# Attention scores in a tuned attention and two-FFN kernel: 64 row by 32 column matmuls in four corners of the array

## The chip, the cores and the metric

The kernel runs on one core of a Trainium2 chip. The core has a matrix engine (TensorE, PE in the profile, with its weight loads as PEld), three engines for elementwise work (VectorE or DVE, ScalarE or ACT, GpSimd or POOL), and SyncE (SP), which here only issues the transfers between main memory (HBM) and on-chip memory (SBUF). Matmuls write to PSUM, which holds 8 banks of 128 partitions by 512 float32 values. The metric is the device time of one execution in microseconds (us).

## The reference

The attention is in chunks of 32 queries. Each chunk sees 8 memory slots, 16 positions to the left, its own 32 and 8 to the right, 64 keys in all. Two feed-forward layers follow, on 3072 tokens of width 512.

```python
for c in range(S // 32):
    k_full = concatenate([mem_k, k[c_start - 16 : c_end + 8]])      # 64 keys, cut at the ends
    scores = scale * q_c @ k_full.T                                 # 32 x 64 per head and chunk
    a = exp(scores - max(scores)); a = a / (sum(a) + 1e-9)
    out_c = a @ v_full
x = attn_out.reshape(3072, 512)
x = relu(x @ moe_w_in) ** 2 @ moe_w_out                             # 512 -> 2048 -> 512
x = silu(x @ w_gate) * (x @ w_val) @ w_out                          # 512 -> 1536 -> 512
```

There are 4 batches, 8 heads, 768 positions and a head width of 64. The inputs are float32.

## The kernel before

The attention is cut into 24 units. A unit is 128 positions of one batch (4 chunks) with all 8 heads, so 32 pairs of a head and a chunk. The host lays out queries, keys (already windowed to 64 per chunk) and values as one block of 128 partitions by 1024 values (512 KB) for each unit. The query block holds two heads on its partitions, 64 rows each, and the columns of a pair of heads are laid out as a block diagonal: 32 columns that are zero in the lower 64 rows and 32 columns that are zero in the upper 64. One matmul of 128 rows by 64 columns thus gives the scores of two heads of a chunk at once, because the zeros keep the two heads apart.

A unit goes through these steps, each a method of `Unit`:

- `__init__` issues the transfers of `q`, `k`, `v` on SP (L525).
- `scores` (L529, matmul in L544) is 16 float32 matmuls into one PSUM bank. Even ones write the partitions 0 to 63, odd ones 64 to 127, so the stationary operands alternate between two column halves of the array.
- `weigh` is the softmax: maximum (L573), subtraction (L578) and sum (L589) on VectorE, the exponential on ACT (L585), the scaling (L603) on POOL or VectorE.
- `turn_pe` (L644, for the first 8 units) or `turn` (L622) transposes the weights into a block-diagonal buffer.
- `mixing` (L673) is the weighted sum, 16 float32 matmuls of the same tile shape as those of the scores.
- `leave` splits the result into a high and a low float32r part (L467, L474) for the first layer.

From the tenth unit on, the weighted sum of one unit and the scores of the next are one planned step: `scores(after)` calls that unit's `mixing()` first. The first layer (L852) and the output of the first layer (L879) are full-size matmuls (128 by 128, 512 moving columns, 12 for each block). The units are spread among them up to about 410 us. After that the second layers (L1108, L1245) follow, without attention.

The order of the work on each engine is not written out by hand. `Plan.run` simulates the engines with costs that are given with every step (`{"PE": 1.16}` for scores alone, `{"PE": 2.2}` with a weighted sum) and with a cost `move` for the bytes of a transfer, and sets the instructions in the order in which this simulation starts them. So a changed `move` can change the order on every engine. Transfers stand in one queue on SP; each waits for the eighth before it.

Of the kernel before, what the change touches and what calls it, by code (L numbers as in the profile page):

```python
# [17 lines left out]
P = 128  # L18
B, H, S, D = 4, 8, 768, 64
CH, LEFT, RIGHT, NMEM = 32, 16, 8, 8  # L20
WIN = NMEM + LEFT + CH + RIGHT
UPB = S // P
NU = B * UPB
# [293 lines left out]
def rate(nbytes):  # L317
    return nbytes / 370e3
# [3 lines left out]
def tile_chunked_attention_two_ffn(ctx: ExitStack, tc, qd, kd, vd, w1, w2, wo2, out):  # L322
# [63 lines left out]
    def at(b):  # L386
        name, n = home(b)
        if name in ("RP", "W1"):
            return wide[name, n]
        if name == "R" and n >= sizes["R"]:  # L390
            n -= sizes["R"]
            if n < 2 * sizes["RP"]:
                return wide["RP", n // 2][:, 1024 * (n % 2) : 1024 * (n % 2) + 1024]
            n -= 2 * sizes["RP"]
            return homes["X"][n // 4][:, 1024 * (n % 4) : 1024 * (n % 4) + 1024]
        return homes[name][n]
# [121 lines left out]
    class Unit:  # L518
        def __init__(self, u, pool, start):
            self.u, self.start = u, start  # L520
            self.q, self.k, self.v = (pl.buf(pool, n) for n in "qkv")
            srcs = [(self.q, qd), (self.k, kd), (self.v, vd)]
            for b, src in srcs:
                pl.op(
                    {"SP": 0.4}, lambda b=b, src=src: nc.sync.dma_start(out=at(b), in_=src[u]),  # L525
                    (), (b,), move=rate(524288),
                )

        def scores(self, after=None):  # L529
            u, sc = self.u, pl.buf("PS", "sc")  # L530
            self.sc = sc
            mixing, reads, writes = after.mixing() if after else (None, (), ())

            def run():
                if mixing:
                    mixing()
                q = at(self.q).rearrange("p (s m c q) -> p s m c q", s=2, m=2, c=4)
                k = at(self.k).rearrange("p (s m c k) -> p s m c k", s=2, m=2, c=4)
                o = at(sc).rearrange("p (s f m k) -> p s f m k", s=2, f=2, m=2)
                for p in range(4):  # L540
                    s, m = p // 2, p % 2
                    for ci in range(4):
                        f, par = ci // 2, ci % 2
                        nc.tensor.matmul(  # L544
                            o[64 * par : 64 * par + 64, s, f, m, :], q[:, s, m, ci, :],
                            k[:, s, m, ci, :], start=True, stop=True,
                        )

            pl.op(
                {"PE": 2.2 if after else 1.16}, run, (self.q, self.k, *reads), (sc, *writes), tail=0.2  # L550
            )

            def edge(r, f, a, b):
                o = at(sc).rearrange("p (s f m k) -> p s f m k", s=2, f=2, m=2)
                nc.vector.memset(o[r : r + 64, :, f, :, a:b], NEG)

            if u % UPB == 0:
                pl.op({"DVE": 0.11}, lambda: edge(0, 0, NMEM, NMEM + LEFT), (), (sc,))
            if u % UPB == UPB - 1:
                pl.op({"DVE": 0.11}, lambda: edge(64, 1, WIN - RIGHT, WIN), (), (sc,))  # L560
# [910 lines left out]
def _layout(q, k, v, mem_k, mem_v, moe_w_in, moe_w_out, moe2_w_gate, moe2_w_val, moe2_w_out):  # L1471

    f = np.float32
    nch = S // CH

    def windows(a, mem):
        pad = np.zeros((B, H, LEFT + S + RIGHT, D), f)
        pad[:, :, LEFT : LEFT + S] = a
        w = np.empty((B, H, nch, WIN, D), f)
        for c in range(nch):  # L1480
            w[:, :, c, :NMEM] = mem
            w[:, :, c, NMEM:] = pad[:, :, c * CH : c * CH + WIN - NMEM]
        return w

    kw, vw = windows(k, mem_k), windows(v, mem_v)

    q8 = q.reshape(B, 2, 2, 2, UPB, 4, CH, D)
    qz = np.zeros((B, UPB, 2, D, 2, 2, 4, 2, CH), f)
    for hh in range(2):
        qz[:, :, hh, :, :, :, :, hh, :] = q8[:, :, :, hh].transpose(0, 3, 6, 1, 2, 4, 5)  # L1490
    k8 = kw.reshape(B, 2, 2, 2, UPB, 4, WIN, D)
    kk = k8.transpose(0, 4, 3, 7, 1, 2, 5, 6)
    v8 = vw.reshape(B, 2, 2, 2, UPB, 4, WIN, D)
    vv = v8.transpose(0, 4, 2, 6, 3, 1, 5, 7)

    def cols(w, nf):
        return w.reshape(KC, P, nf, P).transpose(2, 1, 0, 3).reshape(nf, P, KC * P)

    w1 = np.concatenate([cols(moe_w_in, NF1), moe_w_out.reshape(NF1, P, DM)], axis=2)
    w2 = np.stack([cols(moe2_w_gate, NF2), cols(moe2_w_val, NF2)], axis=1)  # L1500

    wo2 = moe2_w_out.reshape(NF2 // 2, 2, P, 2, DM // 2).transpose(0, 3, 2, 1, 4)
    return {
        "q": qz.reshape(NU, P, 1024),
        "k": kk.reshape(NU, P, 1024),
        "v": vv.reshape(NU, P, 1024),
        "w1": w1.view(np.int64),
        "w2": w2.view(np.int64),
        "wo2": np.ascontiguousarray(wo2).reshape(NF2 // 2, 2, P, DM).view(np.int64),
    }  # L1510
# [19 lines left out]
```

## Time and profile before

| | us |
|---|---|
| median of 3 runs | 1105.41 |
| lowest, highest | 1105.08, 1106.93 |
| the profiled execution's own time | 1106.09 |
| span of its trace | 1104.3 |
| PE busy | 1082.3 (98%) |
| VectorE busy | 860.0 (78%) |
| ACT busy | 594.1 (54%) |
| HBM read, written | 227.02 MB, 81.26 MB |

The span is the time from the first to the last instruction of the program on the core; the execution's own time has some 1.8 us around it. A busy share is an average over the span. Matmuls are pipelined, so the duration of a single one in the trace is longer than the time by which it delays the next, and what a block of them costs is read from start to start.

### The profile page before, as it was taken

What the parts mean: (1) busy time and instruction counts of PE and PEld (TensorE: products, weight loads), DVE (VectorE), ACT (ScalarE), POOL (GpSimd) and SP (SyncE); (2) the same over time, 40 slices, a digit from 0 to 9 for tenths busy, and PEclk for the clock granted to TensorE, in tenths of its full rate; (3) what the DMA queues carried; (4) which work ended last, traced back from release to release, by engine and by line L of the source; (5) the groups of instructions that cost most, each with busy time, mean ns of one, the idle gap of its engine ahead of it and who ended that gap; (6) DMA issues with size and microseconds to landing.
All of it is one profiled execution on the core that took longest, in us unless ns stands there. A gap on an engine that the chain in (4) does not pass through costs nothing.

```text
span 1104.3 us, 17051 instructions
## 1 busy us (share of the span) xinstructions
PE 1082.3 (98%) x6044; PEld 892.0 (81%) x6044; DVE 860.0 (78%) x1540; ACT 594.1 (54%) x1010; POOL 126.5 (11%) x106
## 2 busy tenths in 40 slices
PE   5899999999999999999999999999999999999998
PEld 4778888888888888888888888888888887888886
DVE  6999878878879999778997667998769854534981
ACT  4888554554556566556654344564566633333650
POOL 2113101112011222001300000102310000000000
PEclk9899999999999999999999999999999999999999
DMA  9953487888889889999868999996998578655552
GB/s 362 409 222 113 134 278 242 296 294 300 306 277 344 288 285 342 393 344 348 290 225 266 404 406 395 328 357 224 358 335 298 161 241 307 213 195 172 190 169 99
DMA packets 133669, 309.42 MB, mean 280 GB/s; under 512 B 13136, under 2 KB 50000, under 8 KB 133584
## 3 DMA queue, kind: packets, MB, share of 16 engines
q1 hardware_dynamic: 133584, 308.33, 78.9%
q8 instruction: 48, 0.79, 0.3%
q14 instruction: 37, 0.30, 0.1%
HBM read 227.02 MB, written 81.26 MB: 279 GB/s over the span
## 4 chain that ended last, share of the span: by engine, by line
PE 95%; DMA 2%; ACT 1%; DVE 1%; issue 0%; SPq 0%; ACTq 0%
PE ps L1108 37%; PE ps L1245 22%; PE ps L852 16%; PE ps L879 15%; PE ps L673 2%; PE ps L544 2%; DMA rp0float<-in_w 1%; DMA s<-in_q 1%; ACT f L765 0%; SPq L525 0%; DVE u L486 0%; PE ps L644 0%; ACT f L772 0%; DVE f L486 0%; DVE rp3float32r L815 0%
## 5 line engine op out<-in xcount | busy, mean ns | idle before, releaser
L495 ACT ACTIVATE t<-ps 128x512 f32<-128x512 f32 x170 | 100.9, 596 | 218.4 <-PE ps L852 102.3
L486 DVE TENSOR_TENSOR t<-t,ps 128x512 f32<-128x512 f32 x72 | 49.1, 686 | 42.0 <-PE ps L1108 38.1
L622 DVE STREAM_TRANSPOSE a<-t 32x128 f32<-32x128 f32 x256 | 77.4, 303 | 4.3
L495 ACT ACTIVATE t<-t 128x512 f32<-128x512 f32 x72 | 45.3, 632 | 57.8 <-DVE t L486 57.4
L486 DVE TENSOR_TENSOR u<-u,u 128x512 f32<-128x512 f32 x70 | 48.2, 711 | 0.1
L474 POOL TENSOR_TENSOR r<-t,r 128x512 fp32r<-128x512 f32 x21 | 29.8, 1420 | 147.8 <-ACT r L467 107.8
L467 ACT ACTIVATE f<-f 128x512 fp32r<-128x512 f32 (+1 forms) x60 | 32.4, 546 | 15.3 <-DVE f L486 10.2
L474 DVE TENSOR_TENSOR f<-f,f 128x512 fp32r<-128x512 f32 (+1 forms) x52 | 32.7, 631 | 9.6 <-ACT f L467 9.2
L474 DVE TENSOR_TENSOR r<-t,r 128x512 fp32r<-128x512 f32 x32 | 22.1, 689 | 22.6 <-ACT r L467 22.5
L486 DVE TENSOR_TENSOR u<-ps,t 128x512 f32<-128x512 f32 x26 | 17.9, 689 | 26.5 <-PE ps L1108 24.9
L495 ACT ACTIVATE u<-ps 128x512 f32<-128x512 f32 x45 | 26.7, 595 | 20.6 <-PE ps L1108 20.3
L866 ACT ACTIVATE t<-t 128x512 f32<-128x512 f32 x56 | 35.3, 630 | 1.3
L467 ACT ACTIVATE r<-t 128x512 fp32r<-128x512 f32 x53 | 33.3, 629 | 1.5 <-DVE t L869 0.2
L486 DVE TENSOR_TENSOR u<-ps,u 128x512 f32<-128x512 f32 x34 | 23.4, 689 | 9.4 <-PE ps L1108 8.8
L585 ACT ACTIVATE t<-t 128x512 f32<-128x512 f32 x24 | 15.1, 630 | 22.3 <-DVE t L578 22.3
L673 PEld LDWEIGHTS ps<-a,a 128*64 128x64 f32 x640 | 20.3, 138 | 6.7 <-issue 4.9
L673 PE MATMUL ps<-a,a 128*64 128x64 f32 x640 | 23.0, 225 | 0.0
L544 PE MATMUL ps<-a,a 128*64 128x64 f32 x640 | 22.3, 223 | 0.0
L802 DVE CUSTOM_DVE_ANT_0 f<-f,f 128x2048 uint16<-128x2048 uint16 (+1 forms) x17 | 22.0, 1294 | 0.3
L544 PEld LDWEIGHTS ps<-a,a 128*64 128x64 f32 x640 | 20.4, 138 | 1.8 <-issue 1.4
L474 POOL TENSOR_TENSOR rp9float32r<-u,rp9float32r 128x512 fp32r<-128x512 f32 x2 | 5.9, 2972 | 127.2 <-ACT rp9float32r L467 115.9
L467 ACT ACTIVATE x<-u 128x512 fp32r<-128x512 f32 x26 | 16.3, 626 | 7.6 <-PE ps L1245 4.2
(836 smaller groups left out, 3096.9 us busy)
## 6 DMA issues: line engine op xcount, KB each, us to landing
tma<-f SPq DMA_DIRECT2D x31, 512.0 KB, 5.8
f<-in_w SPq DMA_DIRECT2D x21, 512.0 KB, 5.5
a<-in_q SPq DMA_DIRECT2D x20, 512.0 KB, 5.6
a<-in_k SPq DMA_DIRECT2D x20, 512.0 KB, 6.7
a<-in_v SPq DMA_DIRECT2D x20, 512.0 KB, 4.3
rp0float32r<-tma SPq DMA_DIRECT2D x14, 512.0 KB, 6.2
rp3float32r<-tma SPq DMA_DIRECT2D x12, 512.0 KB, 5.9
rp2float32r<-tma SPq DMA_DIRECT2D x11, 512.0 KB, 6.6
```

What stands on the lines that cost most here:

```text
L467: lambda: nc.scalar.activation(out=dst(HI), in_=src(), func=AF.Copy),
L474: eng.tensor_tensor(out=dst(LO), in0=src(), in1=dst(HI).bitcast(F32), op=ALU.subtract)
L486: eng.tensor_tensor(out=out[1](), in0=x[1](), in1=y[1](), op=op)
L495: nc.scalar.activation(out=out[1](), in_=x[1](), func=func)
L544: nc.tensor.matmul(o[64 * par : 64 * par + 64, s, f, m, :], q[:, s, m, ci, :], k[:, s, m, ci, :], start=True, stop=True,)
L622: nc.vector.transpose(out=o[g : g + 32, hh, :, :, m, :].rearrange("k s (f c) q -> k s f c q", c=2)[:, :, :, par, :], in_=a[r : r + 32, :, ...
L673: nc.tensor.matmul(o[64 * hh : 64 * hh + 64, 2 * s : 2 * s + 2, CH * ci : CH * ci + CH], a[:, hh, s, ci, :], b[:, hh, s, ci].rearrange("p ...
L852: nc.tensor.matmul(at(hp), w1of("in", i, a)[:, k * P : k * P + P], x[:, b, k, :], start=(n == 0), stop=(n == len(terms) - 1),)
L866: nc.scalar.activation(out=at(h), in_=at(h), func=AF.Square)
L879: nc.tensor.matmul(at(accs[m]), w1of("out", i, a)[:, m * P : m * P + P], at(h2)[:, 512 * b : 512 * b + 512], start=(i == 0 and n == 0), st ...
L1108: nc.tensor.matmul(at(bank), at(w[slot])[:, o : o + P], at(r[i, n])[:, 512 * b : 512 * b + 512], start=(first and n == 0 and m == 0), stop ...
L1245: nc.tensor.matmul(at(bank[i][n]), at(w[i][g // 2])[:, o : o + P], at(r)[:, 512 * b : 512 * b + 512], start=(first and m == 0), stop=(g == ...
```

## The change

The query block loses its zeros. It is now 128 partitions by 512 values (256 KB): the 64 rows of one head on the upper partitions, those of the other below, 32 columns for each chunk. The 16 score matmuls become 32, one for each head and chunk, with 64 rows and 32 columns. `tile_position=(r, g)` places each in one of four pieces of the array: rows 0 or 64, columns 0, 32, 64 or 96, so that the four that follow each other lie at (0, 0), (64, 32), (0, 64) and (64, 96). The scores land where they landed before. The planner's cost for the bytes of a query block is halved; its costs for the score step are as before.

```diff
             for b, src in srcs:
                 pl.op(
-                    {"SP": 0.4}, lambda b=b, src=src: nc.sync.dma_start(out=at(b), in_=src[u]),
-                    (), (b,), move=rate(524288),
+                    {"SP": 0.4}, lambda b=b, src=src: nc.sync.dma_start(out=at(b)[:, : src.shape[-1]], in_=src[u]),
+                    (), (b,), move=rate(262144 if src is qd else 524288),
                 )
...
-                q = at(self.q).rearrange("p (s m c q) -> p s m c q", s=2, m=2, c=4)
+                q = at(self.q)[:, :512].rearrange("p (s m c q) -> p s m c q", s=2, m=2, c=4)
                 k = at(self.k).rearrange("p (s m c k) -> p s m c k", s=2, m=2, c=4)
                 o = at(sc).rearrange("p (s f m k) -> p s f m k", s=2, f=2, m=2)
-                for p in range(4):
-                    s, m = p // 2, p % 2
-                    for ci in range(4):
-                        f, par = ci // 2, ci % 2
-                        nc.tensor.matmul(
-                            o[64 * par : 64 * par + 64, s, f, m, :], q[:, s, m, ci, :],
-                            k[:, s, m, ci, :], start=True, stop=True,
-                        )
+                for n in range(32):
+                    (s, m), f, par, hh = divmod(n // 8, 2), n // 4 % 2, n // 2 % 2, n % 2
+                    r, g = 64 * hh, 64 * par + 32 * hh
+                    nc.tensor.matmul(
+                        o[g : g + 32, s, f, m, :], q[r : r + 64, s, m, 2 * f + par, :],
+                        k[r : r + 64, s, m, 2 * f + par, :], start=True, stop=True,
+                        tile_position=(r, g),
+                    )
...
-    qz = np.zeros((B, UPB, 2, D, 2, 2, 4, 2, CH), f)
-    for hh in range(2):
-        qz[:, :, hh, :, :, :, :, hh, :] = q8[:, :, :, hh].transpose(0, 3, 6, 1, 2, 4, 5)
+    qq = q8.transpose(0, 4, 3, 7, 1, 2, 5, 6)
...
-        "q": qz.reshape(NU, P, 1024),
+        "q": qq.reshape(NU, P, 512),
```

The order on PE moves with it. This is its head before the change, from behind the third score block on. A row is a line of the kernel, the operation, output from inputs, the size of the output, and how often; L544 (L543 in the changed kernel) are the scores, L644 transposes, L673 weighted sums, L852 the first layer, `s` and `a` the tiles of queries, keys and values.

```order
L644 MATMUL ps_91<-ident,t_77 128x128 x4
L544 MATMUL ps_92<-s_193,s_192 64x64 x16
L673 MATMUL ps_93<-a_67,s_194 64x2x32 x16
L644 MATMUL ps_94<-ident,t_78 128x128 x4
L673 MATMUL ps_95<-a_68,s_195 64x2x32 x16
L644 MATMUL ps_88<-ident,t_79 128x128 x4
L644 MATMUL ps_89<-ident,t_80 128x128 x4
L673 MATMUL ps_90<-a_67,s_196 64x2x32 x16
L673 MATMUL ps_91<-a_68,s_197 64x2x32 x16
L852 MATMUL ps_92<-xx,rp9float32r 128x512 x12
L852 MATMUL ps_94<-xx,rp9float32r 128x512 x12
L544 MATMUL ps_93<-a_70,a_69 64x64 x16
```

And this is the same place on PE now, from the third score block down to the first full-size block.

```order
L543 MATMUL ps_90<-s_191,s_190 32x64 x32
L543 MATMUL ps_91<-s_193,s_192 32x64 x32
L644 MATMUL ps_92<-ident,t_77 128x128 x4
L644 MATMUL ps_93<-ident,t_78 128x128 x4
L673 MATMUL ps_94<-a_67,s_194 64x2x32 x16
L673 MATMUL ps_95<-a_68,s_195 64x2x32 x16
L644 MATMUL ps_88<-ident,t_79 128x128 x4
L644 MATMUL ps_89<-ident,t_80 128x128 x4
L673 MATMUL ps_90<-a_67,s_196 64x2x32 x16
L673 MATMUL ps_91<-a_68,s_197 64x2x32 x16
L543 MATMUL ps_92<-a_70,a_69 32x64 x32
L852 MATMUL ps_93<-xx,rp9float32r 128x512 x12
```

The fourth score block has moved ahead of the first transpose, and the fifth, which stood behind two blocks of L852, ahead of the first of them. The next place is a weighted sum with the scores behind it, on PE in the second token block of the first layer, before:

```order
L879 MATMUL ps_95<-r_63,rp5float32r 128x512 x3
L673 MATMUL ps_89<-a_67,a_70 64x2x32 x16
L544 MATMUL ps_91<-a_69,a_68 64x64 x16
L852 MATMUL ps_93<-x_66,rp6float32r 128x512 x12
L879 MATMUL ps_94<-r_64,rp6float32r 128x512 x3
```

And now:

```order
L879 MATMUL ps_89<-r_63,rp5float32r 128x512 x3
L673 MATMUL ps_95<-a_67,a_70 64x2x32 x16
L543 MATMUL ps_91<-a_69,a_68 32x64 x32
L852 MATMUL ps_88<-x_66,rp6float32r 128x512 x12
L879 MATMUL ps_92<-r_64,rp6float32r 128x512 x3
```

Nothing has moved here; the two blocks that had one shape now have two.

## Rows read from the trace of the kernel before

**Rows 1.** The page: span, busy times by engine, chain by engine

```profile
span 1104.3 us, 17051 instructions
PE 1082.3 (98%) x6044; PEld 892.0 (81%) x6044; DVE 860.0 (78%) x1540; ACT 594.1 (54%) x1010; POOL 126.5 (11%) x106
PE 95%; DMA 2%; ACT 1%; DVE 1%; issue 0%; SPq 0%; ACTq 0%
```

**Rows 2.** Table of stretches over the whole span

```profile
core 0: us, PE busy (x) PEld busy (x) DVE busy (x) ACT busy (x) POOL busy (x), PEclk, DMA share, GB/s
0.00:8.00 8.00, 0.00 (x0) 0.00 (x0) 1.82 (x4) 2.50 (x3) 2.48 (x8) 1.00 0.70 252
8.00:28.00 20.00, 13.94 (x272) 12.01 (x272) 15.87 (x30) 9.77 (x16) 3.83 (x6) 1.00 1.03 406
28.00:40.00 12.00, 10.25 (x61) 8.09 (x62) 11.08 (x14) 9.11 (x13) 0.00 (x0) 0.72 1.02 409
40.00:80.00 40.00, 38.46 (x223) 30.77 (x222) 38.44 (x48) 36.40 (x49) 6.71 (x5) 1.00 0.79 308
80.00:410.00 330.00, 330.00 (x2459) 272.49 (x2458) 283.99 (x611) 188.17 (x315) 57.90 (x52) 1.00 0.75 260
410.00:612.00 202.00, 202.00 (x893) 167.27 (x892) 174.61 (x290) 117.35 (x209) 24.16 (x16) 1.00 0.89 318
612.00:1104.30 492.30, 487.67 (x2144) 401.42 (x2142) 334.14 (x549) 230.82 (x410) 31.45 (x20) 1.00 0.77 268
```

**Rows 3.** The score line L544 on PE: count, durations in ns, starts

```profile
L544 PE MATMUL ps<-a,a x640: 222/222/270, 37.9 to 388.8; 128*64 128x64 f32 x160
L544 PE MATMUL ps<-s,s x128: 222/314/369, 8.1 to 16.6; 128*64 128x64 f32 x128
```

**Rows 4.** Timeline of PE around one weighted sum and score block

```profile
start us, us, engine line op out<-in xcount [idle before <-releaser]
140.62 2.88 PE L852 MATMUL ps<-x,rp0float32r 128*128 128x512 f32 x12
143.34 2.88 PE L879 MATMUL ps<-r,rp0float32r 128*128 128x512 f32 x12
146.16 1.15 PE L673 MATMUL ps<-a,a 128*64 128x64 f32 x32
147.14 1.10 PE L544 MATMUL ps<-a,a 128*64 128x64 f32 x32
148.17 3.02 PE L852 MATMUL ps<-x,rp1float32r 128*128 128x512 f32 x12
151.02 1.30 PE L879 MATMUL ps<-r,rp1float32r 128*128 128x512 f32 x5
```

**Rows 5.** Records started by 20.44, 20.47, 20.53 us; by 146.165 us

```profile
20.34 0.28 PE L673 MATMUL ps<-a,s 128*64 128x64 f32 x2 [1.47 <-DVE a L653]
20.34 0.34 PE L673 MATMUL ps<-a,s 128*64 128x64 f32 x4 [1.47 <-DVE a L653]
20.34 0.39 PE L673 MATMUL ps<-a,s 128*64 128x64 f32 x6 [1.47 <-DVE a L653]
146.15 0.14 PEld L673 LDWEIGHTS ps<-a,a 128*64 128x64 f32 x2 [0.35 <-issue]
146.16 0.28 PE L673 MATMUL ps<-a,a 128*64 128x64 f32 x2
```

**Rows 6.** Timeline of PE from 7 to 40 us

```profile
8.08 1.98 PE L544 MATMUL ps<-s,s 128*64 128x64 f32 x32 [8.08 <-DMA s<-in_k]
10.65 1.98 PE L544 MATMUL ps<-s,s 128*64 128x64 f32 x32 [0.59 <-DMA s<-in_k]
13.21 1.73 PE L544 MATMUL ps<-s,s 128*64 128x64 f32 x32 [0.58 <-DMA s<-in_k]
...
20.34 1.15 PE L673 MATMUL ps<-a,s 128*64 128x64 f32 x32 [1.47 <-DVE a L653]
...
22.91 0.63 PE L644 MATMUL ps<-ident,t 128*128 128x128 f32 x4 [0.83 <-DVE t L603]
...
25.78 1.15 PE L673 MATMUL ps<-a,s 128*64 128x64 f32 x32 [1.09 <-DVE a L653]
29.75 8.19 PE L852 MATMUL ps<-xx,rp9float32r 128*128 128x512 f32 x24 [2.82 <-ACT xx L467]
```

**Rows 7.** Waits of PE: up to 80 us, behind it the last two

```profile
PE ps L852 <- DVE rp2float32r L815: 1.0, 1, 1.0
PE ps L852 <- DVE rp3float32r L815: 0.4, 1, 0.4
PE ps L852 <- DVE rp4float32r L815: 0.2, 1, 0.2
...
PE ps L1108 <- DVE rp9float32r L474: 0.2, 1, 0.2
PE ps L1108 <- ACT a L495: 0.2, 1, 0.2
```

**Rows 8.** Three stretches of the start, columns as in rows 2

```profile
7.00:17.00 10.00, 7.47 (x132) 6.69 (x132) 7.50 (x15) 3.06 (x5) 1.51 (x3) 1.00 1.03 415
10.00:28.00 18.00, 12.02 (x242) 10.19 (x240) 14.76 (x28) 9.14 (x15) 3.83 (x6) 1.00 1.03 404
29.75:35.00 5.25, 5.25 (x12) 4.13 (x13) 5.18 (x8) 2.58 (x3) 0.00 (x0) 0.50 1.03 410
```

**Rows 9.** The chain that ended last, up to 40 us: start, duration, what

```profile
4.61 9.74 DMA s<-in_q
14.35 0.02 issue
14.37 12.62 DMA rp0float<-in_w
...
27.07 1.12 ACT f L765
28.19 1.03 ACT f L772
29.22 0.49 ACT xx L467
```

## The prediction

> **What bounds the kernel now.** I read the page first: TensorE (PE) is busy 98% of a span of 1104.3 us, and the chain of work that ended last is 95% PE [rows 1]. An average can hide stages, so the table of stretches comes next [rows 2]. It shows three parts. Up to 80 us PE has holes: 8.00 us before its first matmul, 6.06 us between 8 and 28, 1.75 us and 1.54 us after that. From 80 to 612 us it has none, and in the rest 4.63 us are open, nearly all of them behind the last matmul. So what happens in the first 40 us counts by what is late there, and from 80 us on every nanosecond that PE gains or loses arrives in the total one for one. Of the 24 score blocks, 4 stand in the start and 20 later; those of the tiles `a` start between 37.9 and 388.8 us [rows 3].
>
> Next, one score block closely. Each of its 16 matmuls is two records in the trace, so a block is 32 records [rows 3]. Where the block follows the weighted sum (L673, same tile shapes) it runs from 146.16 to 148.17 us together with it [rows 4]. The score row lasts 1.10 us and its last record 0.222 us, so the 32 records start within 0.88 us. They do not start evenly: after a wait two records have started by 20.44 us, four by 20.47, six by 20.53 [rows 5]. So two start together, and 0.88 us is 15 steps of about **58 ns**, two records a step. The matmuls alternate between two column halves of the array. The reading that fits is that both halves work side by side and each takes one record per 58 ns.
>
> **The change, part by part.** It halves the rows and the columns of a score matmul (64 by 32 instead of 128 by 64) and doubles their number: 64 records a block instead of 32. The moved columns, 64, stay. So a record should hold its piece of the array as long as before, and the whole question is how many pieces work at once.
>
> 1. *The matmuls.* With four corners side by side a block is 64/4 = 16 steps of 58 ns = 0.93 us, just what it is now: the zeros that go were multiplied in rows that cost no time. The steps have a second part. In the first block 32 records last 1.98 us, the last of them 0.314 us [rows 3, 6]; over 15.5 steps that is 107 ns a step, and half of it, 53.7 ns, leaves some 4.3 ns of the 58 that do not shrink with the clock. If these belong to the records and not to the step, four records add another 8.6 - 4.3 = 4.3 ns, over 16 steps 0.07 us a block, over 24 blocks 1.7 us; if to the step, nothing. No row tells which: I take half, **+0.9 us** (0 to 1.7).
>
> 2. *Changes of the tile shape.* Now the weighted sum and the scores share a shape and follow each other with nothing lost: from 146.16 to 147.14 is 0.98 us, 16 steps and 0.05 us of a slow first one. Going into and out of that shape costs. The full-size block at 143.34 us takes 2.82 us to the next start and not the 2.72 us of its forerunner, and with the slow first step that is 0.14 us; out of it the score row takes 1.03 us instead of 0.93, and the full-size block behind it 2.85 us instead of 2.72, 0.23 us [rows 4]. After the change the scores have a shape of their own, so a change of shape stands between weighted sum and scores as well. The program has 55 changes of shape before and 68 after, by its order. A change from 128x64 to 64x32 isn't in this trace. I take the price of going in, 13 x 0.14 = **+1.8 us** (0, if it is no real change, to 13 x 0.23 = 3.0). The Trainium skill, "TensorEngine Tiling (Array Packing)", section Tiling Modes, Key Properties, says that changing the tiling mode, and not merely the tile, drains TensorE. The trace agrees where it can, 0.14 and 0.23 us at a change and none between two blocks of one shape; by the page the 13 are paid, which is the 1.8 us.
>
> 3. *The queries' transfers.* A query block falls from 512 to 256 KB. From 80 us on PE waits 0.4 us in all, and for no transfer [rows 7]; there the bytes cost nothing before and save nothing. In the start they do count. The DMA engines are full at 415 GB/s between 7 and 17 us [rows 8], so 262144 bytes are 0.63 us. The first score block waits for keys until 8.08 us, and the next two start 2.57 and 2.56 us apart, one query and one key block each [rows 6]; that becomes 7.45 us and steps of 1.94. Further on the chain runs over the transfer of the weights `rp0`, which land at 26.99 us, then over ACT (L765, L772, L467) to the first full matmul at 29.75 [rows 9]. Four query blocks stand ahead of `rp0` in the queue, 2.5 us. But VectorE is busy 14.76 of the 18 us from 10 to 28 us [rows 8], with the softmax and the copies of the same units, and PE waits for it there too (1.47, 0.83 and 1.09 us [rows 6]). What is late next is VectorE. It starts 0.63 us earlier for certain, and at best all its 3.24 us of holes close. I take **-2.0 us** (-0.6 to -3.2). That holds behind 40 us as well: the weights that PE waits for there (1.0, 0.4 and 0.2 us [rows 7]) come from the same transfers and VectorE.
>
> 4. *The order.* The planner sees cheaper queries and sets some work otherwise. At the start all four score blocks now stand ahead of the first transpose, and the fifth moves ahead of the first full matmul. Moved blocks cost on PE what they cost before, since none is added; what they hide is the wait before 29.75 us, 1.1 us out of 2.82. It is in the -2.0. A granted clock of 0.50 between 29.75 and 35.00 us [rows 8] makes 24 full-size matmuls last 8.19 us [rows 6], where twelve take 2.72 [rows 4]: 2.6 us lost. Other holes ahead of it could remove that or add as much; I take no change, and keep 2.6 us either way for the range.
>
> The sum against the profiled execution's own 1106.09 us: 1106.1 + 0.9 + 1.8 - 2.0 = 1106.8 us. The median of the runs, 1105.41, lies 0.7 us below that execution, so the forecast is **1106 us**, no change that can be told.
>
> **The rivals.** *Two at a time (slower).* The corners don't all work at once: of the matmuls queued in turn for four corners only two are ever active, as now. Then 64 records are 32 steps of 58 ns, 1.86 us, and 0.93 us more for each of the 20 later blocks is 18.6 us. In the start a slow block takes 32 x 107 ns = 3.4 us, more than the 1.94 us between keys, so PE sets the pace there and the gain of part 3 is lost, and about 1.4 us more. 1105.4 + 18.6 + 1.8 + 1.4 = **1127 us**. It decides as soon as fewer than four records share a step. For it: no row shows more than two active, and the two records of one matmul follow each other on the same corner. Against it: if those two had to run one after the other in the order written, the first two records of a block could not both have started by 20.44 us [rows 5]; the array seems to take from the halves independently. The Trainium skill, "TensorE: Matmul & The Clock Gate", Part 3, What overlaps and what doesn't, states that matmuls start and end strictly in program order. By that rule the second record of one corner would hold back the next corner, and this rival would come true; the pairs of rows 5 do not look like it.
>
> *The supply of instructions.* Four corners need 4 weight loads and 4 matmuls per 58 ns. The trace shows no more than half of that over a block, 32 of each in about 0.93 us [rows 4]. Twice the supply can't be excluded, nor that the present one is the limit, which gives the 1127 us again. In the middle, 22 ns a record, a block takes 1.4 us: 20 x 0.47 = 9.4 us, and with 1.8 for the shapes and half the gain of the start 1105.4 + 9.4 + 1.8 - 1.0 = **1116 us**. Against it: the head of a block starts two loads and two matmuls between 146.15 and 146.165 us [rows 5], so bursts at least are quick. The same page, Back-to-back issue gap, gives a floor of about 25 ns from matmul to matmul however small; as an estimate from it a block would be 64 x 25 ns = 1.6 us. The 29 ns mean of a record here neither breaks nor proves that floor.
>
> *The start gives more.* Chain and VectorE both move up by the full 3.2 us, the stretch at half clock falls away (2.6 us), and the new change of shape costs nothing: 1105.4 - 5.8 = **1100 us** (with 0.9 for the records, 1100.5). For it: the DMA engines are full throughout the start. Against it: it needs all three.
>
> **How the numbers follow.** Forecast 50%, two at a time 23%, supply 17%, more from the start 10%. Two runs of this kernel can tell 0.2% apart, 2.2 us. Within the forecast's own case (1101 to 1112 with the ends of its terms and the clock) I put 0.06 below that bound, 0.32 within, 0.12 above. With the rivals: faster 0.06 + 0.10 = 0.16; same 0.32 + 0.01 = 0.33; slower 0.12 + 0.23 + 0.16 = 0.51. The forecast alone is the likeliest single case, though slower outweighs it in sum. The range has to take in the supply and two at a time: **1101 to 1128 us**.
>
> **What would show it.** Right, if a score row (64 records) of a late unit spans about 1.1 to 1.2 us and four records start per step; 2.1 us says two at a time, in between the supply. The gap between weighted sum and scores prices the change of shape: 0.14 us expected beyond a step. The first full matmul should start near 27.8 us instead of 29.75, and behind 80 us PE should still wait for nobody. The forecast is wrong if PE's busy time over 80 to 410 us has grown by over 4 us, or if new waits stand there.

## The result, and the profile after

The changed kernel takes 1111.67 us (median of 4 runs, 1110.49 to 1112.51) against 1105.46 us before, a ratio of 1.0053 with an interval of 1.0036 to 1.0070: half a per cent slower. The forecast was 1106 us and no change. The time lies inside the range, near the upper end of the forecast's own case.

The page of the kernel after, as [rows 1]: span, busy times, the chain that ended last by engine.

```profile
span 1108.7 us, 18586 instructions
PE 1084.1 (98%) x6812; PEld 891.0 (80%) x6812; DVE 854.9 (77%) x1530; ACT 594.7 (54%) x1011; POOL 137.5 (12%) x115
PE 90%; DMA 6%; DVE 2%; ACT 1%; issue 1%; SPq 0%; POOL 0%; ACTq 0%; POOLq 0%
```

PE has 1.8 us more to do and the span is 4.4 us longer, so 2.6 us of the loss are idle time. POOL has 11 us more to do, and the chain, 95% PE before, now leaves PE more often. The table of stretches, as [rows 2], says where PE stands idle.

```profile
core 0: us, PE busy (x) PEld busy (x) DVE busy (x) ACT busy (x) POOL busy (x), PEclk, DMA share, GB/s
...
40.00:80.00 40.00, 35.18 (x299) 27.50 (x298) 37.12 (x45) 34.22 (x44) 12.97 (x7) 1.00 0.67 262
80.00:410.00 330.00, 330.00 (x2968) 271.28 (x2967) 281.55 (x602) 185.46 (x311) 55.06 (x55) 1.00 0.71 243
410.00:612.00 202.00, 201.36 (x887) 165.82 (x886) 169.09 (x283) 119.12 (x212) 30.47 (x18) 1.00 0.88 317
```

From 40 to 80 us PE had 1.54 us of holes; it now has 4.82. From 80 to 410 us it has none, as before, and from 410 to 612 us 0.64 us are new. The waits of PE between 28 and 125 us name them, as [rows 7] (total, times, longest).

```profile
PE ps L852 <- DVE rp4float32r L815: 1.7, 1, 1.7
PE ps L852 <- DVE rp1float32r L815: 1.4, 1, 1.4
PE ps L852 <- DVE rp2float32r L815: 1.0, 1, 1.0
PE ps L852 <- DVE rp0float32r L815: 1.0, 1, 1.0
PE ps L852 <- DVE rp3float32r L815: 0.7, 1, 0.7
PE ps L852 <- ACT xx L467: 0.6, 1, 0.6
```

All but the last are for the first layer's weights, whose last step, L815, runs on VectorE: 5.8 us for `rp0` to `rp4`, where before it was 1.6 us for three of them [rows 7]. The wait for `xx` has fallen from 2.82 [rows 6] to 0.6 us.

The score blocks themselves did what the forecast said. One late step of weighted sum and scores on PE, as [rows 4], and the records that have started by 260.60 and 260.65 us, as [rows 5]:

```profile
start us, us, engine line op out<-in xcount [idle before <-releaser]
259.41 1.15 PE L673 MATMUL ps<-a,a 128*64 128x64 f32 x32
260.49 1.10 PE L543 MATMUL ps<-a,a 64*32 64x64 f32 x64
261.52 1.66 PE L879 MATMUL ps<-r,rp2float32r 128*128 128x512 f32 x6
...
260.49 0.32 PE L543 MATMUL ps<-a,a 64*32 64x64 f32 x8
260.49 0.37 PE L543 MATMUL ps<-a,a 64*32 64x64 f32 x12
```

64 records take the 1.10 us that 32 took, four more start in the next 0.05 us, and the four corners work side by side. From the weighted sum to the next full-size matmul it is 2.11 us, against 2.01 in [rows 4] (148.17 less 146.16). So a fused step lost about 0.10 us and nothing else; that explains 1.5 us over the 15 fused steps, and not 6.

### The profile page after: what moved, and what is told of

It is laid out like the page before. It is cut to its first block, busy times and chain, and to the rows that moved or that the text cites. A ratio compares the mean times of both kernels' runs of the same rounds, so it can differ in the third digit from the quotient of the medians.

```text
span 1108.7 us, 18586 instructions
## 1 busy us (share of the span) xinstructions
PE 1084.1 (98%) x6812; PEld 891.0 (80%) x6812; DVE 854.9 (77%) x1530; ACT 594.7 (54%) x1011; POOL 137.5 (12%) x115
## 4 chain that ended last, share of the span: by engine, by line
PE 90%; DMA 6%; DVE 2%; ACT 1%; issue 1%; SPq 0%; POOL 0%; ACTq 0%; POOLq 0%
PE ps L1108 35%; PE ps L1245 21%; PE ps L879 15%; PE ps L852 15%; PE ps L673 2%; PE ps L543 2%; DMA rp1float<-in_w 1%; DMA rp4float<-in_w 1%; DMA s<-in_v 1%; DMA rp8float<-in_w 1%; DMA u<-yd 1%; DMA rp7float32r<-tma 1%; DMA s<-in_q 0%; DMA tmb<-f 0%; DVE u L486 0%
## 5 line engine op out<-in xcount | busy, mean ns | idle before, releaser
L474 POOL TENSOR_TENSOR r<-t,r 128x512 fp32r<-128x512 f32 x27 | 42.1, 1558 | 165.8 <-ACT r L467 157.4
L467 ACT ACTIVATE f<-f 128x512 fp32r<-128x512 f32 (+1 forms) x71 | 38.4, 544 | 23.0 <-DVE f L486 13.0
L474 DVE TENSOR_TENSOR f<-f,f 128x512 fp32r<-128x512 f32 (+1 forms) x66 | 41.7, 633 | 8.3 <-ACT f L467 6.2
L474 DVE TENSOR_TENSOR r<-t,r 128x512 fp32r<-128x512 f32 x26 | 18.2, 699 | 19.6 <-ACT r L467 19.5
L673 PEld LDWEIGHTS ps<-a,a 128*64 128x64 f32 x640 | 20.3, 138 | 6.8 <-issue 4.2
L673 PE MATMUL ps<-a,a 128*64 128x64 f32 x640 | 23.0, 225 | 0.0
L594 POOL TENSOR_SCALAR m<-m 128x8 f32<-128x8 f32 x18 | 8.4, 464 | 111.7 <-DVE m L589 111.5
L543 PE MATMUL ps<-a,a 64*32 64x64 f32 x1280 | 21.9, 217 | 0.3 <-DMA a<-in_k 0.3
L802 DVE CUSTOM_DVE_ANT_0 f<-f,f 128x2048 uint16<-128x2048 uint16 (+1 forms) x17 | 21.4, 1263 | 0.2
L543 PEld LDWEIGHTS ps<-a,a 64*32 64x32 f32 x1280 | 18.8, 107 | 2.8 <-issue 1.4
L573 DVE TENSOR_REDUCE m<-ps 128x8 f32<-128x512 f32 x24 | 16.4, 683 | 5.2 <-PE ps L543 5.0
```

The source lines that it names most:

```text
L467: lambda: nc.scalar.activation(out=dst(HI), in_=src(), func=AF.Copy),
L474: eng.tensor_tensor(out=dst(LO), in0=src(), in1=dst(HI).bitcast(F32), op=ALU.subtract)
L543: nc.tensor.matmul(o[g : g + 32, s, f, m, :], q[r : r + 64, s, m, 2 * f + par, :], k[r : r + 64, s, m, 2 * f + par, :], start=True, stop=True,
L673: nc.tensor.matmul(o[64 * hh : 64 * hh + 64, 2 * s : 2 * s + 2, CH * ci : CH * ci + CH], a[:, hh, s, ci, :], b[:, hh, s, ci].rearrange("p ...
```

## The experiments

Two theories stood at the start. **Order**: the planner, told of cheaper queries, set VectorE's and GpSimd's work otherwise, and that costs the time. **Corners**: the matmuls, their changes of shape or their transfers cost it. The measure beside the time is how much later a given first-layer block starts than in the trace of before: the L852 blocks that start there at 123.00 us and at 403 us, and the last matmul. All values are in us; each median stands against a median of before in the same comparison (1105.46 for after, 1105.68 for e0 to e3, 1105.44 for e4 to e7, 1105.21 for e8 to e11). The comparisons of the experiments ran on three different chips. In the last three columns only the differences between runs count, since the trace of before is itself late at 123 us (see "3, the transfers" further down).

| kernel | median | ratio, interval | at 123 | at 403 | last |
|---|---|---|---|---|---|
| after | 1111.67 | 1.0036 to 1.0070 | +1.0 | +2.5 | +4.7 |
| e0 changed, again | 1110.99 | 1.0034 to 1.0058 | +1.2 | +2.7 | +4.1 |
| e1 corners, old order | 1105.86 | 0.9997 to 1.0016 | -3.0 | -1.5 | -0.4 |
| e2 new order alone | 1110.87 | 1.0034 to 1.0059 | +2.3 | +2.3 | +4.7 |
| e3 corners, old bytes | 1106.64 | 0.9997 to 1.0018 | -2.3 | -0.8 | -0.4 |
| e4 old start, new later | 1107.33 | 1.0006 to 1.0026 | -3.1 | -1.7 | +0.5 |
| e5 new start, old later | 1109.25 | 1.0027 to 1.0054 | +1.4 | +2.8 | +4.5 |
| e6 corners in start only | 1104.42 | 0.9980 to 0.9999 | -2.3 | -2.3 | -2.0 |
| e7 one corner in a row | 1161.23 | 1.0499 to 1.0542 | +18.8 | +53.6 | +53.7 |
| e8 no GpSimd split | 1110.60 | 1.0034 to 1.0060 | -0.1 | +1.4 | +3.8 |
| e9 small step on VectorE | 1109.64 | 1.0029 to 1.0056 | +0.8 | +2.2 | +3.9 |
| e10 scores split | 1109.49 | 1.0023 to 1.0048 | -2.4 | +1.0 | +3.4 |
| e11 two corners | 1119.49 | 1.0109 to 1.0146 | +0.1 | +12.6 | +13.1 |

**e0, the changed kernel once more**, unedited, beside the next three.

> The changed kernel once more, for a second trace and more times. Both theories expect its median again, 1111.7 us (1110.4 to 1112.6). The trace of the first profiled execution accounts for +4.4 us of span, and the median is 6.2 us over that of before: a second trace may show where the other 1 to 2 us come and go; I expect it in the first 80 us, where PE waits for weights that VectorE and GpSimd prepare, and not in the score blocks.

It repeats, time and stretch by stretch. Between 123 and 403 us both traces lose 1.5 us evenly, about 0.10 us for each fused step; the rest is lost ahead of 123 us and behind 403.

**e1, the change without its order.** The planner is told the old bytes; matmuls and transfers are the changed ones.

```diff
-                    (), (b,), move=rate(262144 if src is qd else 524288),
+                    (), (b,), move=rate(524288),
```

> The matmuls in four corners and the 256 KB queries as in the change, but the planner is told the old bytes, so every engine gets the order of the kernel before, instruction for instruction. Theory 'order': of the 6.2 us only the changes of tile shape belong to the corners, 16 x 0.10 = 1.6 us, and the rest to the order that the planner made of the cheaper transfers; 1105.5 + 1.6 = 1107 us, less what the bytes give in the start (0 to 2 us): 1105 to 1107.5. Rival 'corners': the new matmuls and transfers cost the 6 us themselves, in any order: 1111 to 1112.

5.1 us of the change's time are gone with one number that no instruction reads. The time can't be told from before. What the trace gains at 403 us does not all arrive: at about 930 us PE waits 1.0 us, and the last matmul is 0.4 us early instead of 1.5.

**e2, the order without the change.** The kernel before with the changed kernel's cost, so zeros, 128x64 matmuls and 512 KB, set in the new order.

```diff
-                    (), (b,), move=rate(524288),
+                    (), (b,), move=rate(262144 if src is qd else 524288),
```

> The kernel before with its 128 by 64 matmuls and 512 KB queries; only the planner is told half the bytes for a query, so every engine gets the order of the changed kernel. Theory 'order': 1105.5 + 6.2 - 1.6 = 1110 us (1108 to 1112; the queries land later than this order reckons, which can add up to 2.5 us in the start). Rival 'corners': 1105.5, no change.

It is as slow as the changed kernel, and loses nothing from 123 to 403 us, since it has no change of shape there. Not all of its 2.3 us at 123 us need be the order: its blocks are still 512 KB, and PE waits 2.2 us for a block of keys for which the changed kernel waits 0.26. With e1, which has no such open end, this decides for the order.

**e3, e1 with the query block padded to 512 KB.**

```diff
-        "q": qq.reshape(NU, P, 512),
+        "q": np.concatenate([qq.reshape(NU, P, 512), np.zeros((NU, P, 512), f)], axis=2),
```

> As e1 (four corners, old order), but a query block is padded to 512 KB and moved whole, so the transfers cost what they did. The difference to e1 is what the saved bytes give in the old order. By part 3 of the prediction 2.0 us (0.6 to 3.2): e3 near e1 + 2. If VectorE sets the pace of the start whatever lands earlier, as the trace of the changed kernel suggests: e3 = e1 within 0.7 us.

The bytes are worth 0.7 us at 123 us, and 0.8 us by the medians, whose intervals overlap.

**e4 and e5, which part of the order.** The new bytes are told for the later units only, or for the first 8 only.

```diff
-                    (), (b,), move=rate(262144 if src is qd else 524288),
+                    (), (b,), move=rate(262144 if src is qd and u >= 8 else 524288),   # e4
+                    (), (b,), move=rate(262144 if src is qd and u < 8 else 524288),    # e5
```

> The changed kernel, but the planner is told the old bytes (512 KB) for the queries of the first 8 units and the new ones (256 KB) for the rest. Transfers and matmuls are those of the change. On TensorE the first 200 or so rows of the order are those of the kernel before, and behind about 120 us the order is a new one, as in the changed kernel. Theory 'order of the start': the new order costs its time before 125 us, on VectorE and GpSimd between 28 and 66 us. Then the first-layer blocks at 123 us start some 3 us earlier than in the trace of before (as with the old order throughout), 1.5 us earlier at 403 us, and what the later order adds from there (1.3 us between 403 and 540 us with the changed order) is all that is left: 1106 to 1107.5 us. Rival 'order of the later part': the cost of 5 us comes from behind 120 us, then about 1110 us.

> The mirror image: the planner is told the new bytes for the first 8 units only. The head of the order is the changed kernel's, behind about 120 us it differs from it and is close to the old one. Theory 'order of the start': first-layer blocks at 123 us start 1 us later than in the trace of before, 2.5 us later at 403 us, and 2 to 4 us at the end: 1109 to 1110.5 us. Rival 'order of the later part': 1106 us.

Both come out as the theory said. The new start costs 4.4 us at 123 us (e5 against e1) and 3.4 us in the medians (3.6 with each against its own before). The new later order costs 1.5 us in the medians (e4 against e1; 1.7 with each against its own before), whose intervals overlap, but its trace shows where: two waits of PE between 420 and 560 us, which after has as well, and e1 and e5 have not.

```profile
PE ps L1108 <- ACT t L495: 0.4, 1, 0.4
PE ps L1108 <- DVE u L486: 0.2, 1, 0.2
```

In e4 five L1108 records there start 785, 335, 337, 637 and 335 ns behind the one ahead, instead of 227: 1.3 us in all.

**What stands on VectorE and GpSimd in the start.** The timeline of VectorE in the kernel after, from the last step of `rp0` to that of `rp1`, then GpSimd's from 36 to 66 us:

```profile
34.99 1.22 DVE L815 TENSOR_TENSOR rp0float32r<-f,rp0float32r 128x1024 fp32r<-128x1024 f32 x1
36.13 1.22 DVE L794 SCALAR_TENSOR_TENSOR f<-rp1float,f 128x1024 int32<-128x1024 int32 x1
37.27 0.68 DVE L573 TENSOR_REDUCE m<-ps 128x8 f32<-128x512 f32 x1
37.87 2.07 DVE L802 CUSTOM_DVE_ANT_0 f<-f,f 128x2048 uint16<-128x2048 uint16 x1
39.86 1.78 DVE L786 TENSOR_SCALAR f<-f 128x1024 int32<-128x1024 int32 x1
41.56 0.68 DVE L578 TENSOR_TENSOR t<-ps,m 128x512 f32<-128x512 f32 x1
42.16 1.21 DVE L815 TENSOR_TENSOR rp1float32r<-f,rp1float32r 128x1024 fp32r<-128x1024 f32 x1
...
37.55 1.30 POOL L474 TENSOR_TENSOR r<-t,r 128x512 fp32r<-128x512 f32 x1 [15.57 <-ACT r L467]
39.67 1.42 POOL L474 TENSOR_TENSOR r<-t,r 128x512 fp32r<-128x512 f32 x1 [0.82 <-ACT r L467]
45.14 2.25 POOL L474 TENSOR_TENSOR r<-t,r 128x512 fp32r<-128x512 f32 x1 [4.05 <-ACT r L467]
47.48 0.23 POOL L594 TENSOR_SCALAR m<-m 128x8 f32<-128x8 f32 x1
57.97 4.98 POOL L474 TENSOR_TENSOR r<-t,r 128x512 fp32r<-128x512 f32 x1 [10.27 <-ACT r L467]
```

Two steps of the fifth unit's softmax (L573, L578) stand ahead of the last step of `rp1`, where in e1 below only L573 does; its scores moved ahead of the first full-size matmul. L802 and L786 last 2.07 and 1.78 us while GpSimd works, where they last 1.22 and 0.69 us elsewhere. The same stretch in e1, with the old order:

```profile
34.70 1.22 DVE L815 TENSOR_TENSOR rp0float32r<-f,rp0float32r 128x1024 fp32r<-128x1024 f32 x1
35.83 1.22 DVE L802 CUSTOM_DVE_ANT_0 f<-f,f 128x2048 uint16<-128x2048 uint16 x1
36.97 0.68 DVE L474 TENSOR_TENSOR r<-t,r 128x512 fp32r<-128x512 f32 x1
37.57 0.69 DVE L779 TENSOR_SCALAR f<-f 128x1024 f32<-128x1024 f32 x1
38.17 0.69 DVE L573 TENSOR_REDUCE m<-ps 128x8 f32<-128x512 f32 x1
38.77 1.22 DVE L815 TENSOR_TENSOR rp1float32r<-f,rp1float32r 128x1024 fp32r<-128x1024 f32 x1
```

From L815 to L815 it is 4.07 us there and 7.17 us in after. (With the old order GpSimd stretches two operations as well, to 1.73 and 2.00 us between 41 and 45 us, but it has two L474 in this part and not four.) The granted clock is not what differs here: it is 0.50 in after from 15.3 to 22.1 us, and e1 has no such stretch in its start, but L815 of `rp0` starts only 0.29 us later in after, and the rest comes behind it. The L815 of `rp4`, first in after with what stands ahead of it, then in e1:

```profile
59.45 2.35 DVE L802 CUSTOM_DVE_ANT_0 f<-f,f 128x2048 uint16<-128x2048 uint16 x2
62.38 1.13 DVE L474 TENSOR_TENSOR r<-t,r 128x512 fp32r<-128x512 f32 x1 [0.58 <-ACT r L467]
63.43 1.21 DVE L815 TENSOR_TENSOR rp4float32r<-f,rp4float32r 128x1024 fp32r<-128x1024 f32 x1
...
59.42 1.23 DVE L815 TENSOR_TENSOR rp4float32r<-f,rp4float32r 128x1024 fp32r<-128x1024 f32 x1
```

It ends at 64.64 us in after and at 60.64 in e1. The lateness is 3.4 us at `rp1`, 2.3 at `rp2`, 2.6 at `rp3` and 4.0 at `rp4`: part of it is made up again, and 1.4 us are new between `rp3` and `rp4`, where in after both L802, of `rp4` and of `rp5`, stand ahead and VectorE waits 0.58 us for ACT. The next two runs ask how much of these 4 us is GpSimd.

**e8, the first four L474 of GpSimd on VectorE**, at the same place in the program.

```diff
+    lows = []
...
+            lows.append(e)
-            eng = nc.gpsimd if e == "POOL" else nc.vector
+            eng = nc.gpsimd if e == "POOL" and lows.count("POOL") > 4 else nc.vector
```

> The changed kernel in its own order, but the first four L474 that the planner gave to GpSimd (at 37.55, 39.67, 45.14 and 57.97 us in the trace of after) run on VectorE, at the place in the program where they were issued. Everything else is unchanged. Theory 'GpSimd': what the new order costs in the start is GpSimd working beside VectorE (two VectorE operations stretched by 0.85 and 1.09 us at 38 to 41 us) and standing ahead of the L594 that VectorE waits 1.51 us for. VectorE takes over four operations of about 0.6 us each (2.4 us) and is rid of these 3.4 us and of 1.0 us around 62 us: it is 2 us earlier at rp4, the first-layer block at 123 us starts 1 us earlier than in the trace of before instead of 1.0 us later, and the time is about 1109 us. Rival 'VectorE's own order' (the fifth unit's softmax ahead of rp1, rp5's steps ahead of rp4's last): the 2.4 us come on top and nothing goes, the block at 123 us starts up to 3 us later than before, about 1112.5 us.

VectorE's timeline in e8, whose lines stand 3 further down (L805 for L802, L789 for L786):

```profile
38.84 1.22 DVE L805 CUSTOM_DVE_ANT_0 f<-f,f 128x2048 uint16<-128x2048 uint16 x1
39.98 0.69 DVE L789 TENSOR_SCALAR f<-f 128x1024 int32<-128x1024 int32 x1
...
46.52 0.20 DVE L602 RECIPROCAL m<-m 128x8 f32<-128x8 f32 x1
```

The stretched operations are back at 1.22 and 0.69 us, and the reciprocal waits for nobody, so GpSimd was their cause. But the gain is 1.1 us at 123 us (-0.1 for +1.0), half of what the theory said, and the medians show none: e8 is 1.0047 of its before, e0 1.0046 of its own. Both theories hold in part. With the four L474 on VectorE about 1 of the 4 us is gone, though VectorE has 2.4 us more to do. The other 3 us stay: from L815 of `rp0` to that of `rp1` (35.37 and 41.78 us in e8) it is still 6.41 us for 4.07 in e1, with nothing stretched, because L794 of `rp1`, L786, L578 and one more L474 stand there, and L779 does not.

**e9, the L594 of the fifth unit on VectorE.**

```diff
-                (nc.gpsimd if e == "POOL" else nc.vector).tensor_scalar(
+                (nc.gpsimd if e == "POOL" and self.u != 4 else nc.vector).tensor_scalar(
```

> The changed kernel in its own order, but the L594 of the fifth unit (0.23 us on GpSimd, behind an L474 of 2.25 us, VectorE waits 1.51 us for it at 47.74 us) runs on VectorE. Nothing else moves. If that wait is on the path, rp2's L815 ends 1.3 us earlier (49.5 instead of 50.84), and the block at 123 us starts up to 1.3 us earlier: 1109.7 us. If what is late next (GpSimd's L474 of 4.98 us at 57.97 and the ACT step L467 that VectorE waits for at 62.38) holds rp4 where it is, rp2 is earlier and the block at 123 us is not: 1111 us.

Neither reading was right. The wait of 1.51 us went, and `rp2` came only 0.2 us earlier (50.62 for 50.84), because the small step itself now took the time. VectorE in e9:

```profile
46.22 1.27 DVE L594 TENSOR_SCALAR m<-m 128x8 f32<-128x8 f32 x1
47.52 0.20 DVE L599 RECIPROCAL m<-m 128x8 f32<-128x8 f32 x1
```

8 values on a partition in 1.27 us: it ran until GpSimd's L474 (45.19 to 47.46 us) was over. So the queue behind L474 was not what VectorE lost; that it is the time shared with L474 fits the trace. The median, 1109.64, fits the 1109.7 us of the first reading by luck: the trace shows that its mechanism isn't there.

**e6, corners for the first 8 units only**, in the old order. The other units keep zeros and 128x64 matmuls.

```diff
-            srcs = [(self.q, qd), (self.k, kd), (self.v, vd)]
+            srcs = [(self.q, qd if u < NC else qzd), (self.k, kd), (self.v, vd)]
...
+                for p in range(4 if u >= NC else 0):      # the 16 matmuls of before
...
-                for n in range(32):
+                for n in range(32 if u < NC else 0):
```

> The old bytes are told to the planner for all units, so the order is that of the kernel before. The first 8 units have the query block without zeros (256 KB) and the scores in four corners; units 8 to 23 have the query block with zeros (512 KB) and 128x64 matmuls of the weighted sum's shape, as before the change. Theory 'a change of shape is paid in every fused step': the gain of the start stays (3 us against the trace of before at 123 us), and the 0.10 us that each step of weighted sum and scores lost with the corners is not lost: still about 3 us (2.5 to 3.2) at 403 us, 1.5 us better than with corners throughout, so 1104.0 to 1105.0 us unless a later wait takes it. Rival 'the loss of 1.5 us between 123 and 403 us is not the change of shape': it goes on, about 1.5 us gain left at 403 us, 1105.9 us.

From 123 to 403 us it loses nothing (-2.3 at both), so the 1.5 us there are the change of shape. At 1104.42 us it is the fastest of all, 0.1% under before, by an interval that only just leaves 1 out. At 123 us its trace is no better than e3's, although its first 8 units move the bytes of e1: the granted clock was 0.50 from 14.4 to 17.8 us, its fourth score block took 1.93 us for 1.10, and its first weighted sum started at 17.62 us for 16.86 in e1. That the later units keep the longer transfers is no loss to it: e1 and e3 are 0.7 us apart at 123 us and still 0.7 at 403.

**e10, one more change of shape in each fused step.** Half of the scores stand ahead of the weighted sum, half behind it.

```diff
-                if mixing:
-                    mixing()
...
                 for n in range(32):
+                    if n == 16 and mixing:
+                        mixing()
```

> Corners, 256 KB and the order of the kernel before, but in each of the 15 fused steps half of the score matmuls stand ahead of the weighted sum and half behind it. The matmuls are the same; each fused step has one change of tile shape more (full size, 64x32, 128x64, 64x32, full size). Theory 'a change of shape costs': 0.125 us for the added one, up to 0.22: 15 x 0.125 to 0.22 = 1.9 to 3.3 us more than the 1105.9 us of the unsplit kernel, 1107.7 to 1109.2 us; in the trace the first-layer blocks lose 0.23 to 0.32 us for each fused step instead of 0.10. Rival 'the 0.10 us is a cost of the score block itself': unchanged, 1106 us and 0.10 us a step.

The fused step in e10 on PE:

```profile
257.58 0.65 PE L543 MATMUL ps<-a,a 64*32 64x64 f32 x32
258.17 1.15 PE L673 MATMUL ps<-a,a 128*64 128x64 f32 x32
259.25 0.65 PE L543 MATMUL ps<-a,a 64*32 64x64 f32 x32
259.83 1.65 PE L879 MATMUL ps<-r,rp2float32r 128*128 128x512 f32 x6
```

2.25 us instead of 2.11, and 0.225 us lost for each step instead of 0.10: the added change costs 0.13 us, and the 15 cost 1.9 us, as expected. Behind 403 us it loses another 2.4 us, which was not expected and puts the median 0.3 us over the expected range. The loss stands at about 930 us, first a wait of PE:

```profile
PE ps L1108 <- ACT rp9float32r L467: 1.7, 1, 1.7
```

In e1 the same wait is 1.0 us, in after 0.8, in e0 0.2, and in before it is not among the waits there. Behind the wait e10 has a granted clock of 0.50 from 930.9 to 934.4 us, where nine full-size matmuls take 3.65 us from start to start (at 0.227 us each it would be 2.04). What sets the wait was not tried and stays open; a comparison of two medians here can carry a microsecond of it.

**e7 and e11, how many corners work at once.** The same 32 matmuls as in e1, issued corner by corner (e7), or round two corners and then round the other two (e11).

```diff
-                    (s, m), f, par, hh = divmod(n // 8, 2), n // 4 % 2, n // 2 % 2, n % 2
+                    (par, hh), (s, m), f = divmod(n // 8, 2), divmod(n // 2 % 4, 2), n % 2      # e7
+                    par, (s, m), f, hh = n // 16, divmod(n // 4 % 4, 2), n // 2 % 2, n % 2      # e11
```

> The order of the kernel before, query blocks of 256 KB, corners; but the 32 matmuls of a block are issued corner by corner, 8 to a corner, instead of going round the four. The work is the same. Theory 'a corner takes one record per 56 ns and TensorE takes its instructions nearly in the order written': only one corner (at the changes two) works at a time, 16 records a corner and 64 steps of 56 ns, 3.6 us a block instead of 0.93; for 20 blocks 53 us more, about 1159 us. Rival 'the array looks ahead in its queue and finds free corners by itself': a block stays near 0.9 to 1.2 us, about 1106 to 1111 us. In between (the queue reaches some matmuls ahead): 2 us a block, 1127 us.

> Corners, 256 KB and the order of the kernel before, but the 32 matmuls of a block go round two corners only, 16 of them (rows 0 to 63 on columns 0 to 31, rows 64 to 127 on columns 32 to 63), then the other two. If a corner takes one record per 56 ns and TensorE reaches some four records ahead of the order written, as the run with one corner in a row shows, a block's 64 records start within 32 x 56 = 1.79 us, less about 0.1 where the pairs change, instead of 0.88: 20 blocks x 0.8 = 16 us more, about 1122 us. If it is the number of instructions that sets the pace when two corners or more are at work, a block stays near 0.9 to 1.2 us and the time near 1106 to 1111 us.

The score block in e7, then the records that had started by 168.70, 168.84 and 169.04 us, and the block in e11:

```profile
168.14 3.18 PE L543 MATMUL ps<-a,a 64*32 64x64 f32 x64
168.14 0.74 PE L543 MATMUL ps<-a,a 64*32 64x64 f32 x10
168.14 0.91 PE L543 MATMUL ps<-a,a 64*32 64x64 f32 x13
168.14 1.11 PE L543 MATMUL ps<-a,a 64*32 64x64 f32 x20
...
265.76 1.79 PE L543 MATMUL ps<-a,a 64*32 64x64 f32 x64
```

In e7 one record starts per 56 ns up to the 13th; from there seven start in 0.20 us. So a corner takes one record per 56 ns, and the next corner's first record starts beside the 13th of 16, three ahead of its turn. In e11 the second pair likewise starts beside the 13th record of each corner of the first. A reading that fits both is that each corner holds three waiting records, and that the issue stops only at a corner that is full. Each such overlap saves about 0.2 us: e7, with three of them, starts a block's records within 3.0 us instead of 3.6, and e11, with one, within 1.6 instead of 1.8. Behind the first full-size matmul the 20 later blocks lose 41 us in e7 and 14 us in e11, as these 2.1 and 0.7 us a block say. In e7 the four blocks of the start take 5.3 to 5.8 us each and add 12.4 us, which the expectation left out; that its 1159 us lie so near is luck. Round all four, as the change does it, is the right way to write it.

## Why the prediction was right or wrong

*What bounds the kernel.* Right in the main: what PE loses behind 80 us arrives in the total, and what happens ahead of it counts by what is late there. Not one for one, though: of e1's 1.5 us at 403 us only 0.4 reach the last matmul.

*1, the matmuls.* The mechanism was right, four corners side by side in steps of 56 ns. The +0.9 us for a part that belongs to the record was wrong: 16 steps start within 0.88 us with four records a step, as with two [rows 3 to 5]. It is 0. The 4.3 ns behind it are mis-sized as well, since 15 steps are counted in one block and 15.5 in the other; 15 in both leave 3.0 ns. That the first block ran at half the clock, which the halving takes for granted, is not in its rows, which give 1.00 there [rows 8].

*2, changes of the shape.* +1.8 us were forecast, 13 changes at 0.14 us each; between 123 and 403 us e1 lost 1.5 us in 15 fused steps, 0.10 us each, and e6 nothing, and e10's added change cost 0.13. The Trainium skill's page "TensorEngine Tiling (Array Packing)", Tiling Modes, Key Properties, says that a new mode drains the engine; these 0.10 to 0.13 us at each change, and none without, agree with it.

*3, the transfers.* The -2.0 us were too much: the 256 KB are worth 0.7 us (e3 against e1), near the certain end of 0.6. That VectorE would be late next was right. The other 2.3 us that e1 and e3 are ahead at 123 us are not the bytes; they lie in the trace of before, and two things in it are late. Its `rp0` landed 12.6 us after the issue [rows 9], in e3 with the same bytes 10.9 us; ACT waited 1.58 us for it, which it does not in e3, and the first full-size matmul started at 29.75 us for 28.49. Then came the 2.6 us lost at a granted clock of 0.50 [rows 8], where e1 and e3 have 1.00. The clock alone does not do it: e4 has 0.50 from 27.4 to 30.8 us and is 3.1 us ahead all the same. So a wait of 2.82 us for `xx` was in part an accident of the one execution that the prediction read. No such gain shows in the medians, so how often before meets this stays open.

*4, the order.* Here the prediction failed. "Moved blocks cost on PE what they cost before, since none is added; what they hide is the wait before 29.75 us, 1.1 us out of 2.82." The first half is true and was the wrong question: beyond that wait the order was put at nothing. The wait was hidden indeed, 0.6 us for 2.82 (1.5 in e1). But a score block that moves on PE brings its softmax forward on VectorE, the engine that the prediction itself had named as late next, ahead of the weights that PE waits for; and GpSimd got two more L474 there, which held VectorE up. e1 and e2 price it: 5.1 us, of them 3.4 in the start (e5) and about 1.5 behind (e4). The range holds the result by luck, since it was widened for the two slower rivals and the clock and not for this. The listing of PE's order in the part on the change stood before the prediction; VectorE's, where it mattered, did not.

*The rivals.* Two at a time and the supply of instructions are refuted by 64 records within 0.88 us, 14 ns apart in the mean. e11 shows what two at a time would have cost, 1119 us where the rival said 1127, since the records of the next pair start early. The rule of program order, from the Trainium skill's page "TensorE: Matmul & The Clock Gate", Part 3, What overlaps and what doesn't, does not hold across corners: in e7 the next corner's first record starts beside the 13th of 16. Nor does the floor of about 25 ns from matmul to matmul, from the section Back-to-back issue gap of the same page of the Trainium skill, hold across corners: in after the four records of a step, on four corners, start 6 to 8 ns apart, though the 32 matmuls of a block, of two records each, come to 28 ns in the mean. "More from the start" did not come true: of the 3.0 us that e1's trace is ahead at 123 us only 0.7 are the bytes, and its median is that of before. That the slower side got the highest chance was right, for reasons that were not the one.

*What would show it.* The late score row (1.10 us for 1.1 to 1.2), the four records a step and the price of a change (0.10 to 0.13 us for 0.14) were about as said. The first full-size matmul came at 29.47 instead of 27.8 us, and behind 80 us PE waits anew at 447 and 543 us.

## What to carry to other kernels

When a change alters a cost that a scheduler reads, build it twice, once with the old cost: the difference between the two is the order, and here it was 5.1 us, nearly all of the loss. Read the new order on the engine that is late next, not on the one that the change is about. Where only part of the kernel gains from a new tile shape, use it there alone.

## What the runs showed of the hardware

- Four corners of 64 rows by 32 columns each take one record per 56 ns, 64 records in 0.88 us; a corner that is written 16 records in a row still lets the next one start three records early (e7).
- A change between 128x64 and 64x32 costs 0.10 to 0.13 us.
- GpSimd's L474 holds VectorE up: L786 took 1.78 us beside it and 0.69 without it (e8), and a VectorE operation on 8 values a partition 1.27 us, until L474 was over (e9). L474 itself took 1.30 to 4.98 us beside VectorE; that VectorE is the cause was not tested.
